# A retention-plus-GELU-MLP kernel with a build-time planner: smaller attention lead in blocks 0 and 1, a finer cut of the first product, transposes queued in the planner, a new load order

## The chip, the cores and the metric

One NeuronCore of one Trainium2 chip runs the whole program. The metric is the device time of one execution in microseconds (us). Three executions of the kernel before gave a median of 310.16 us (307.47 to 310.43). The profile is of one further execution, which took 309.51 us; its span, from the first to the last profiled instruction, is 307.7 us, so about 1.8 us lie around the span.

## The reference

The inputs are `q`, `k`, `v` of 8 batches x 8 heads x 576 positions x 64, and two weight matrices. First a retention: causal attention without softmax, each score multiplied by a decay that falls with distance. Then an MLP with exact GELU on the 4608 x 512 result.

```
scores = (q @ k^T) / 8
ret    = scores * where(i >= j, gamma[h] ** (i - j), 0)        # gamma[h] = 1 - 2 ** (-5 - h)
x      = (ret @ v), heads side by side: 4608 tokens x 512
h      = x @ w_in                                               # 512 x 2048
out    = (0.5 * h * (1 + erf(h / sqrt(2)))) @ w_out             # 2048 x 512, float32
```

## The kernel before

**Work.** The 4608 tokens are cut into 36 units of 128 tokens (all 8 heads together) and into 9 blocks of 4 units (512 tokens). Block t of the MLP needs the attention results of units 4t to 4t+3. Units 0 to 3 are the first chunks of four sequences; after that, units come in groups of two (the same chunk of two sequences), and each pair of sequences ends with a unit of two half chunks. Unit 10 is such a tail; units 11 and 12 are chunk 1 of the second pair of sequences.

**One unit.** `load` (L213, L217) brings q, k and v from HBM as bf16 by DMAs issued from GpSimd (POOL). q and k are transposed: for units 0 to 7 by TensorE (`turn`, L292, copied out of PSUM by VectorE or ScalarE), for later units by a DMA transpose issued on SyncE (`turn_dma`, L301). `scores` (L314) multiplies them, `masked` (L329, VectorE) applies the causal mask into `ret`. `scaled_v` (L339, VectorE) makes `vh`, v times a decay. `inner` (L351) multiplies `ret` with `vh` into a PSUM bank `o`. `state` (L369) sums k times `vh` over a chunk, and `cross` (L403) adds what earlier chunks contribute. `evacuate` (L423, VectorE) writes the unit's part of `xT`. Unit 2 and 3's tiles are kept aside, so VectorE scales v in the order 0, 1, 4 to 10, 2, 3, 11, 12 and so on.

**The MLP of a block.** `mlp1` (L442) is 64 matmuls of 512 columns (or 128 of 256 in blocks 0 and 1) from `xT` and `w_in`; ScalarE applies GELU into `g` (L448). `mlp2` (L481) is 64 matmuls of 512 columns from `g` and `w_out`, and the result goes out by SyncE's store (L489).

**What sets the order.** Nothing waits on a scheduler on the chip. A planner in Python writes every engine's instructions in a fixed order while the program is built. It keeps a clock per engine (`T`), a due time for each load (`land`), computed in `sw_dma` as one serial stream in which at most eight loads are outstanding, and one for each transposed unit (`s["T", j]`). At each step of its main loop it first calls `fire`, which issues loads (in the order of the list `ORDER`, then `reload`, three loads per unit), puts a `scaled_v` on VectorE as soon as the planner's clock has passed the due time of that v (and six more units than have been finished are not exceeded), and issues DMA transposes as soon as k is due. Then it takes the first attention step that is due, or else the next piece of MLP. If nothing is due before 16 us, it fills the gap with matmuls on zeros (`warm`, L565, and six at the start, L572).

On the chip each engine runs its list in order and waits on semaphores where data are late; the due times are then without effect, but the order that they gave remains. POOL's list holds the loads, SyncE's list the transposes and the stores, VectorE's list masks, `vh` and the evacuations together.

**The lead.** A new group's `scores` may be placed in the second product of a block only before two of the four pieces of each token tile, and only if the number of scored units stays within `4 * t + AHEAD`:

```
elif head is None or head[1] == 0 or head[0] == "2" and 4 <= head[3] <= 8 and head[1] < N_BLK - 1:
    if len(back) == nA - nB and (head is None or nA + len(g) <= 4 * head[1] + AHEAD):
```

With `AHEAD = 11` block 1 may score up to unit 14. The planner's window on MLP work is four runs while block 0 or 1 is at the head; a run is the list of pieces of one column range or of one group of token tiles.

## Time and profile before

| what | value |
|---|---|
| median of 3 executions | 310.16 us (307.47 to 310.43) |
| profiled execution | 309.51 us, span 307.7 us |
| TensorE matmul (PE) | busy 296.8 us, 96% of the span |
| VectorE (DVE) | busy 97.1 us, 32% |
| ScalarE (ACT) | busy 136.0 us, 44% |
| GpSimd (POOL) | busy 114.0 us, 37% |
| granted TensorE clock | 1.00 throughout |
| DMA | 35.76 MB moved, 28 transposes, mean 116 GB/s |
| first useful `mlp1` matmul | at 15.69 us |
| first `mlp1` matmul of block 2 | at 90.52 us |

How to read it: times in the views count from the start of the span. A view by time gives start, duration, engine, line, operation and tile, the number of instructions merged, and in square brackets how long the engine had been idle before and what released it. A busy share near 100% says that an engine has work, not that the work is wanted: the zero matmuls of the first 16 us count as busy. The chain of work that ended last is followed back from the end, from each instruction to what released it; a piece of it named DMA is a wait for a transfer. Idle time of an engine off this chain costs nothing.

### The profile page before, as it was taken

The page shows a single profiled execution, that of the slowest core. Times are in us where ns is not written, and L with a number is a line of the kernel's source. Part 1 is how long each engine was busy: PE and PEld are TensorE (multiplying, and loading weights), DVE is VectorE, ACT ScalarE, POOL GpSimd, SP SyncE. Part 2 cuts the span into 40 slices and gives each one's busy share as a digit, 9 for nine tenths or more (in the row PEclk, how much of TensorE's full clock was granted, in tenths as well). Part 3 has the DMA queues.
Part 4 walks back from the last instruction along what each step waited for, and adds up shares of the span by engine and source line. Part 5 has one row for each costly group of instructions (what it writes and reads, how often), then busy time and mean ns, then how long its engine had stood idle before and what let it go on. Part 6 is the DMA issues. An engine that isn't in the chain of part 4 may idle for free.

```text
span 307.7 us, 5630 instructions
## 1 busy us (share of the span) xinstructions
PE 296.8 (96%) x2354; PEld 158.9 (52%) x2354; DVE 97.1 (32%) x185; ACT 136.0 (44%) x237; POOL 114.0 (37%) x143
## 2 busy tenths in 40 slices
PE   7999999989959999999999999999999999999996
PEld 2488575855424554445445554454446444544445
DVE  6851446334543181018001851073006300400000
ACT  5286154633316622653266226631663166216611
POOL 8987899942348474105311863100000000000000
PEclk9999999999999999999999999999999999999999
DMA  9999999999999999965990999923000110010022
GB/s 142 162 191 183 177 181 214 169 151 136 169 191 186 138 156 174 194 56 86 150 159 2 167 166 174 148 69 104 34 0 36 51 54 0 36 68 34 2 60 76
DMA packets 154042, 35.76 MB, mean 116 GB/s; under 512 B 143009, under 2 KB 149537, under 8 KB 154017
## 3 DMA queue, kind: packets, MB, share of 16 engines
q0 software_dynamic: 116832, 18.10, 83.3%
q1 hardware_dynamic: 36144, 17.05, 28.8%
q8 instruction: 18, 0.29, 0.4%
q10 hardware_dynamic: 1040, 0.26, 0.4%
q14 instruction: 8, 0.06, 0.1%
HBM read 36.70 MB, written 9.44 MB: 150 GB/s over the span
## 4 chain that ended last, share of the span: by engine, by line
PE 70%; DMA 17%; POOL 10%; issue 2%; DVE 0%; ACT 0%; POOLq 0%; DVEq 0%
PE hT L442 31%; PE oT L481 30%; DMA v_ld<-in_v_dram 6%; DMA qk_ld<-in_q_dram 4%; POOL qk_ld L217 4%; DMA w_in<-in_moe_w_in_dram 3%; DMA w_out<-in_moe_w_out_dram 3%; POOL v_ld L217 3%; PE o_ps L351 2%; PE sc L314 2%; DMA qk_ld<-in_k_dram 2%; PE o_ps L403 2%; POOL w_in L191 1%; PE oT L468 1%; POOL dqT L199 1%
## 5 line engine op out<-in xcount | busy, mean ns | idle before, releaser
L442 PE MATMUL hT<-xT,w_in 128*128 128x512 bf16 (+1 forms) x704 | 127.3, 340 | 3.4 <-DVE xT L423 3.2
L481 PE MATMUL oT<-w_out,g 128*128 128x512 bf16 x560 | 126.5, 379 | 0.0
L448 ACT ACTIVATE g<-hT 128x512 bf16<-128x512 f32 x144 | 85.6, 597 | 42.3 <-PE hT L442 42.2
L442 PEld LDWEIGHTS <-w_in 128*128 128x128 bf16 x704 | 68.6, 98 | 60.4 <-issue 3.5
L481 PEld LDWEIGHTS <-g 128*128 128x128 bf16 x560 | 53.5, 98 | 60.4
L329 DVE TENSOR_TENSOR ret<-sc,msk 128x512 bf16<-128x512 f32 x56 | 35.7, 683 | 99.8 <-PE sc L314 99.8
L486 ACT COPY o_sb<-oT 128x512 f32<-128x512 f32 x35 | 20.4, 586 | 89.6 <-PE oT L481 73.0
L217 POOL DMA_DIRECT2D qk_ld<-in_q_dram x31 | 27.8, 898 | 47.0 <-PE u_ps L369 31.5
L217 POOL DMA_DIRECT2D v_ld<-in_v_dram x32 | 28.9, 906 | 8.0 <-DMA qk_ld<-in_q_dram 5.6
L282 ACT CAST u_sb<-u_ps 64x512 bf16<-64x512 f32 x31 | 18.0, 580 | 25.6 <-PE u_ps L369 24.4
L217 POOL DMA_DIRECT2D qk_ld<-in_k_dram x31 | 27.9, 900 | 3.7 <-DMA v_ld<-in_v_dram 2.9
L339 DVE TENSOR_TENSOR vh<-v_ld,dv 128x512 bf16<-128x512 bf16 x36 | 23.4, 682 | 12.4 <-DMA v_ld<-in_v_dram 12.4
L329 DVE TENSOR_TENSOR ret<-sc,near 128x512 bf16<-128x512 f32 x16 | 10.2, 682 | 35.9 <-PE sc L314 35.9
L423 DVE TENSOR_TENSOR xT<-o_ps,dqT 128x512 bf16<-128x512 f32 x28 | 18.1, 682 | 5.7 <-PE o_ps L403 5.7
L314 PE MATMUL sc<-qkT 64*128 64x128 bf16 x288 | 12.8, 223 | 2.4 <-DMA qkT<-qk_ld 2.4
L314 PEld LDWEIGHTS <-qkT 64*128 64x128 bf16 x288 | 8.3, 96 | 6.1 <-DMA qkT<-qk_ld 2.9
L351 PEld LDWEIGHTS <-vh 128*64 128x64 bf16 x224 | 6.7, 109 | 6.8 <-issue 5.9
L280 DVE COPY qkT<-qk_ps 128x512 bf16<-128x512 bf16 x13 | 5.3, 421 | 13.0 <-PE qk_ps L292 12.9
L351 PE MATMUL o_ps<-ret,vh 128*64 128x128 bf16 x224 | 9.3, 222 | 0.0
L403 PE MATMUL o_ps<-qkT,u_sb 128*128 128x128 bf16 (+1 forms) x128 | 9.1, 214 | 0.0
L213 POOL DMA_DIRECT2D v_ld<-in_v_dram x8 | 5.4, 680 | 9.4 <-DMA v_ld<-in_v_dram 3.9
L213 POOL DMA_DIRECT2D qk_ld<-in_q_dram x8 | 5.6, 706 | 4.7 <-DMA v_ld<-in_v_dram 2.2
(51 smaller groups left out, 94.1 us busy)
## 6 DMA issues: line engine op xcount, KB each, us to landing
out_dram<-o_sb SPq DMA_DIRECT2D x31, 256.0 KB, 4.6
v_ld<-in_v_dram POOLq DMA_DIRECT2D x32, 128.0 KB, 8.4
qk_ld<-in_q_dram POOLq DMA_DIRECT2D x31, 128.0 KB, 8.3
qk_ld<-in_k_dram POOLq DMA_DIRECT2D x31, 128.0 KB, 8.1
w_in<-in_moe_w_in_dram POOLq DMA_DIRECT2D x8, 256.0 KB, 7.0
w_out<-in_moe_w_out_dram POOLq DMA_DIRECT2D x8, 256.0 KB, 8.3
out_dram<-o_sb SPq DMA_DIRECT2D x9, 128.0 KB, 3.5
qk_ld<-in_k_dram POOLq DMA_DIRECT2D x8, 64.0 KB, 12.1
```

The source lines that it names most:

```text
L217: nc.gpsimd.dma_start(dst, src[2 * bp + j, :, ci * C:ci * C + C, :].rearrange("h s d -> s h d"))
L282: nc.scalar.copy(dst, src)
L314: nc.tensor.matmul(got[e][1][:, hp, :], lhsT=qkT[sl, 1, hp, :], rhs=qkT[sl, 0, hp, :], start=True, stop=True)
L329: nc.vector.tensor_tensor(r, t, by, op=ALU.mult)
L339: nc.vector.tensor_tensor(vh, loaded[i][1], dv[:, :, ci:ci + 1].to_broadcast([128, H, D]), op=ALU.mult)
L351: nc.tensor.matmul(o[64 * e:64 * e + 64, hp, :], lhsT=vals[:, 2 * hp + e, :], rhs=s["ret"][e][:, hp, :], start=(hp == 0), stop=(ci == 0 an ...
L403: nc.tensor.matmul(o[:, hp, cols], lhsT=u[:, jj, hp, :], rhs=s["qkT"][:, 0, hp, cols], start=False, stop=(hp == HP - 1), skip_group_check= ...
L423: nc.vector.tensor_tensor(dst, o, by, op=ALU.mult)
L442: nc.tensor.matmul(hT[:, m, :], lhsT=w[:, cc, o:o + 128], rhs=xT[:, cc, t * TOK + lo:t * TOK + hi], start=(cc == 0), stop=(cc == N_DM - 1))
L448: nc.scalar.activation(g_tiles[t, m0 // 2][:, m0 % 2:m0 % 2 + n, lo:hi], hT, AF.Gelu)
L481: nc.tensor.matmul(oT, lhsT=g_tiles[t, m // 2][:, m % 2, cols], rhs=w_out_sb[m // 2][:, m % 2, :], start=(m == 0), stop=(m == N_DF - 1))
L486: nc.scalar.copy(o_sb, oT)
```

## The change

Six edits, all in the planner; no instruction's operands change except the widths of the first product.

- `AHEAD` goes from 11 to 9, and 2 is added back for blocks above 1: block 0 may score 9 units and block 1 13; later blocks keep their limit.
- Block 0's first product is cut into 256, 128 and 128 columns instead of 256 and 256, so there are three runs of it in the window.
- The planner's DMA transposes are a serial queue: each takes 3.1 us after the one before and lands 3.4 us later. Before, each landed 8 us after its own issue. A transpose now delays the planner's loads by 1.6 us; before, it was 1.8 us or more.
- The planner's latency of a load goes from 4.95 to 5.2 us, and its TensorE costs are doubled up to 7.5 us (`HOT`), in place of a dearer transpose up to 9 us.
- Eight zero matmuls at the start instead of six, and a new rule for the number of those that fill gaps before 16 us.
- A new load order. k and q of unit 1 change places, v of unit 1 comes before the first weights and the constants, v of units 0 and 2 before q and k of unit 3; k and q of unit 8 come much earlier.

```diff
@@ -69,7 +69,8 @@
     N_LD = 9
     N_QKT = 8
     N_VH = 6
-    AHEAD = 11
+    AHEAD = 9
+    HOT = 7.5
 
     const = ctx.enter_context(tc.tile_pool(name="const", bufs=1))
     ld_pool = ctx.enter_context(tc.tile_pool(name="ld", bufs=N_LD))
@@ -160,6 +161,7 @@
 
 
     sw = [0.0]
+    turned = [0.0]
     flying = []
     dq_done = {1}
     land = {}
@@ -171,7 +173,7 @@
             T["pool"] = max(T["pool"], flying[-8])
         at = T["pool"]
         T["pool"] += issue
-        sw[0] = max(sw[0] + move, at + 4.95 + move - 0.9)
+        sw[0] = max(sw[0] + move, at + 5.2 + move - 0.9)
         flying.append(sw[0])
         return sw[0]
 
@@ -220,8 +222,8 @@
     tiles_of(0)
     land["q", 0], land["k", 0] = 4.5, 4.6
     cast_due = {("q", 0): (loaded[0][0][:, 0], first["q32"]), ("k", 0): (loaded[0][0][:, 1], first["k32"])}
-    ORDER = ("q1 k1 wi0 io v1 q2 k2 q3 k3 v0 v3 wi1 v2 wi2 k4 wi3 wi4 wi5 wi6 q4 v4 wo0 k5 wi7 q5 wo1 wo2 wo3 v5 k6 q6 "
-             "wo4 q7 v8 k7 dq2 wo5 wo6 q8 wo7 v7 dq3 dq4 v6 q9 k10 k9 v9 k8 q10 v10").split()
+    ORDER = ("k1 q1 v1 wi0 io k2 q2 v0 wi1 v2 k3 q3 wi2 wi3 v3 wi4 wi5 wi6 k4 q5 k5 q4 wo0 wo1 wi7 v4 v5 wo2 k6 q6 "
+             "wo3 dq2 k7 q7 wo4 k8 q8 wo5 wo6 dq3 v6 v7 wo7 v8 q9 k9 v9 dq4 q10 k10 v10").split()
 
     def next_order():
         item = ORDER.pop(0)
@@ -267,7 +269,7 @@
         if mode[0] != to:
             T["pe"] += 0.11
             mode[0] = to
-        T["pe"] += dur
+        T["pe"] += dur * (2.0 if T["pe"] < HOT else 1.0)
         return T["pe"] + DRAIN
 
 
@@ -290,7 +292,7 @@
         b, t = bank([128, HP, 128], BF16, "qk_ps")
         for hp in range(HP):
             nc.tensor.transpose(t[:, hp, :], qk[:, jj, 2 * hp:2 * hp + 2, :], ident1)
-        done = pe(0.3 if T["pe"] < 9 else 0.225)
+        done = pe(0.225)
         done = either(0.42, done, s["qkT"][:, jj], t)
         release(b, done + 0.05)
         s["T", jj] = done + SEM
@@ -300,9 +302,10 @@
         s["qkT"] = tr_pool.tile([128, 2, HP, 128], BF16, tag="qkT", name="qkT")
         nc.sync.dma_start(s["qkT"].rearrange("p j hp s -> p (j hp) s"),
                           loaded[i][0].rearrange("p j h d -> p (j h d)"), transpose=True)
-        at = on("sp", 1.3, land["k", i])
-        sw[0] = max(sw[0] + 1.8, at)
-        s["T", 0] = s["T", 1] = at + 8.0
+        at = on("sp", 1.3, max(land["q", i], land["k", i]))
+        turned[0] = max(turned[0], at) + 3.1
+        sw[0] += 1.6
+        s["T", 0] = s["T", 1] = turned[0] + 3.4
 
     def scores(i):
         s = st[i]
@@ -494,8 +497,9 @@
     runs = []
     for t in range(N_BLK):
         if t < 2:
-            for lo in (0, 256):
-                runs.append([("1", t, m, 2, lo, lo + 256) for m in range(0, N_DF, 2)])
+            cuts = (0, 256, 384, 512) if t == 0 else (0, 256, 512)
+            for lo, hi in zip(cuts, cuts[1:]):
+                runs.append([("1", t, m, 2, lo, hi) for m in range(0, N_DF, 2)])
         else:
             runs.append([("1", t, m, 1, 0, TOK) for m in range(N_DF)])
         order = range(4) if t < N_BLK - 1 else (3, 0, 1, 2)
@@ -567,7 +571,7 @@
         release(b, T["pe"])
 
     T["pe"] = 1.3
-    for _ in range(6):
+    for _ in range(8):
         b, t = bank([128, 512], FP32, "warm")
         nc.tensor.matmul(t, lhsT=zeros[:, :128], rhs=zeros, start=True, stop=True)
         release(b, 0.0)
@@ -613,7 +617,7 @@
                 if early or stuck:
                     cand(max(ready, free_time(2)) if ok else 1e9, "A", g, [])
                 elif head is None or head[1] == 0 or head[0] == "2" and 4 <= head[3] <= 8 and head[1] < N_BLK - 1:
-                    if len(back) == nA - nB and (head is None or nA + len(g) <= 4 * head[1] + AHEAD):
+                    if len(back) == nA - nB and (head is None or nA + len(g) <= 4 * head[1] + AHEAD + 2 * (head[1] > 1)):
                         cand(max(ready, free_time(min(n, 8 - len(held))) - 0.3), "A", g, back)
         if nT < N_PE_TR and nT <= nA + 3:
             key = ("qk"[half], nT)
@@ -670,8 +674,8 @@
         if not waits:
             break
         gap = min(waits) - now
-        if now < 16 and gap > 0.35:
-            warm(max(1, int(gap / 0.2158 * (0.5 if now < 9 else 0.8))))
+        if now < 16 and gap > 0.2:
+            warm(max(1, round(gap / (0.43 if now < HOT else 0.23))))
         T["pe"] = max(T["pe"], min(waits))
     assert nX == N_U and not any(runs), (nA, nB, nX, nT, nV, [len(r) for r in runs])
 
```

## The prediction

> **What bounds the kernel now.** I read the busy time by stage first, then the matmul engine's list by time, then the chain of waits. The stages:

> ```profile
> 0.00:15.70 15.70, 13.26 (x99) 5.51 (x100) 11.63 (x43) 6.30 (x16) 14.59 (x23) 1.00 1.72 153
> 15.70:65.50 49.80, 49.63 (x501) 37.02 (x500) 20.29 (x37) 27.54 (x48) 41.52 (x51) 1.00 1.87 183
> 65.50:90.50 25.00, 19.44 (x229) 10.38 (x229) 11.86 (x20) 5.82 (x10) 9.54 (x13) 1.00 1.72 162
> 90.50:305.00 214.50, 214.45 (x1528) 105.95 (x1527) 53.29 (x87) 96.11 (x163) 48.32 (x58) 1.00 0.86 94
> ```

> (Columns: stretch, length, busy time of PE, weight load, DVE, ACT, POOL, then clock, DMA share, GB/s.) From 15.7 to 65.5 and from 90.5 to the end PE has no hole. So the change can win or lose in two places alone: before 15.7, where much of PE's busy time is zero matmuls, and from 65.5 to 90.5, where 5.56 us are idle. It can also make a new hole. The idle time of the third stage, in PE's list:

> ```profile
> 65.53 0.40 PE L314 MATMUL sc<-qkT 64*128 64x128 bf16 x8
> 67.22 0.40 PE L314 MATMUL sc<-qkT 64*128 64x128 bf16 x8 [1.29 <-DMA qkT<-qk_ld]
> ...
> 77.50 0.40 PE L314 MATMUL sc<-qkT 64*128 64x128 bf16 x8 [0.25 <-DMA qkT<-qk_ld]
> ...
> 85.07 0.40 PE L314 MATMUL sc<-qkT 64*128 64x128 bf16 x8 [0.81 <-DMA qkT<-qk_ld]
> 85.40 1.90 PE L481 MATMUL oT<-w_out,g 128*128 128x512 bf16 x8
> 90.52 1.67 PE L442 MATMUL hT<-xT,w_in 128*128 128x512 bf16 x7 [3.22 <-DVE xT L423]
> ```

> Three scores come before their transposes have landed (1.29 + 0.25 + 0.81 = 2.35 us), then block 2 waits 3.22 us for an evacuation. That wait is not the evacuation's own. DVE's list, and the chain of waits:

> ```profile
> 80.29 1.28 DVE L339 TENSOR_TENSOR vh<-v_ld,dv 128x512 bf16<-128x512 bf16 x2
> 89.18 0.69 DVE L339 TENSOR_TENSOR vh<-v_ld,dv 128x512 bf16<-128x512 bf16 x1 [7.61 <-DMA v_ld<-in_v_dram]
> 89.78 1.28 DVE L423 TENSOR_TENSOR xT<-o_ps,dqT 128x512 bf16<-128x512 f32 x2
> ```

> ```profile
> 57.94 13.60 DMA qk_ld<-in_q_dram
> ...
> 72.07 17.08 DMA v_ld<-in_v_dram
> 89.15 0.02 issue
> 89.18 0.04 DVE vh L339
> ...
> 89.78 0.69 DVE xT L423
> 90.48 0.04 issue
> 90.52 13.97 PE hT L442 x64
> ```

> Counting in the order of `scaled_v`, the `vh` at 89.18 is that of unit 16, which block 2 does not need. It stands ahead of the evacuations of units 11 and 12 in DVE's list, and its v landed at 89.15. Block 2 (units 8 to 11) is pegged to the v of unit 16. **This place decides the forecast**: whatever PE gains before it is lost there unless that `vh` moves behind the evacuation of unit 11.

> **The change, part by part.**

> Start. Before the first transpose PE now has 8 zero matmuls and, by the new rule, about 3 more. (The constants move behind v of unit 1, one POOL issue of 0.9 us, so the cast of q on DVE slips from 4.90 to about 5.8.) At the 0.64 us of the row at 1.86 and 2.50, and 0.58 for the last ones, eleven end near 8.0, against 5.57 for the first transpose before: about 2.4 us later. Against it, v of unit 0, whose landing at 14.30 released the first `inner` (14.35), moves up four issues of 0.87 to 0.90 and lands near 12.4. From `inner` to the first product were 15.69 - 14.35 = 1.34 us. With scores, masks (0.685 each) and fillers after the late transposes, `inner` comes near 13.8 and the product near 15.1, 0.6 us earlier. But the weights now land later beside the loads of units 2 and 3 (second near 13.5, third 17.1, fourth 18.4, fifth 20.5, by the 1.3 us spacing of weights and 0.9 of loads in the trace), v of unit 3 near 19.2, and I find PE fully fed only from about 20. Counted by useful work done by then (transposes, scores and 24 or 26 equivalents of 256 columns), the start gains 0.2 us. Bounds: a loss of 2.6 (a planned batch of eight fillers at 0.54 instead of 0.22 each, if the clock is still low at 10 us) and a gain of 1.9 (all that v of unit 0 moves up). I take 0.2, as the fillers after 9.9 ran 0.28 apart.

> [...] Here weight loads of fillers still started 0.64 us apart at 3.78 and 4.42 although PE had worked since 1.20, and the first 0.28 apart came at 9.92. [...]

> Cut of 256, 128, 128. Half of block 0's 13.98 us becomes 128 matmuls of 128 columns. The last tile's L468 shows 32 such in about 1.80 us, 0.0563 each: 7.21 against 6.99, so +0.22 us, spent in the full stage 15.7 to 65.5. GELU pieces go from 16 x 0.597 to 8 x 0.597 + 16 at 0.37 (the copy of 256 columns took 0.37): 10.7 us in some 14, so ACT stays ahead. Sum with the start: nothing.

> Lead. Unit 13 and 14's scores (the pair at 83.86 and 85.07) leave block 1: 0.55 us of PE (16 matmuls of scores, the chain's row for a pair) moves behind the start of block 2's product. If block 2 stays pegged this is +0.55; if not, 0. Their wait of 0.81 goes with them: two blocks later the transposes (landed by 88) are there. The other two waits, 1.54, go if transposes come sooner: k of unit 8 was the last of its group (landed 51.61) and opened the queue at 54.54; it now lands near 41, so its transpose leaves about 12 us earlier, and those of units 9 to 12 start one place of 3.1 to 3.3 us sooner. SyncE's list then has a transpose ahead of the first stores, which cannot hurt at 42 since the first store went at 47.91. Bounds of this part: 0.8 to 2.35 us gained, and I take 1.9.

> The peg. `ORDER` holds the same items up to unit 10 and `reload` goes on as before, so the stream up to v of unit 16 holds the same bytes, in a DMA share that stays above 1.7. Its landing can move only by what shares the engines. From 62.63 to 89.15 landed 12 loads, 8 transposes and 3 stores; at 0.87 a load, 10.4 us; the other 16.1 us fit 1.6 per transpose and 1.1 per store. With PE some 2 us earlier, half a store more falls before it: +0.5 (bounds -1.6, one transpose less, to +3.8, one transpose and two stores more).

> Whether the `vh` still stands in front is settled in the planner's dates, which I added up by hand. They give an order, no time on the chip. Before: v of unit 16 was due at 79.58 (70.58 of loads and five transposes of 1.8), and `inner` and `state` of units 11 and 12 ended at 80.14, so it went in just ahead of `evacuate`. Now the loads sum to 70.83 and a transpose adds 1.6. With five transposes ahead of it the due time is 78.83 and `vh` stays in front; with six it is 80.43, after 80.14, and slips behind the evacuation of unit 11. Five or six hangs on whether the planner's clock takes a step between 55.53 and 56.03, when the transpose of unit 10 is due but v of unit 13 not yet called: 0.5 of a step of 0.87, so 57 to 43 for six, before what I cannot add up exactly (PE's planned clock to about 0.4).

> **The cases.** All from the profiled execution's 309.51.

> A, still pegged (0.47): 309.51 + 0.55 + 0.5 = **310.6**. Start and transpose gains only lengthen the wait at block 2, to about 6 us. Own range 308.5 to 312.

> B, `vh` behind both evacuations (0.25): 309.51 - 3.22 - 1.9 = **304.4**. For it: nothing in DVE's list needs to pass v of unit 16 until block 2's second product, 14 us later.

> B', `vh` between the evacuations of 11 and 12 (0.13): block 2 starts, but unit 12's PSUM bank stays taken until about 90.6, and of eight banks in turn it is wanted after about five pieces of 0.86: 310.6 - 4.3 = **306.3**.

> C, slower (0.15): still pegged, and the v of unit 16 lands later because stores of block 1 and a transpose, released earlier, take the engines first. Place: the wait at the start of block 2; price +3.8 - 0.5 over A: **313.9**. It decides once one more transpose and one more store than I allow land before that v. Against it: SyncE's ninth transpose waited for the k of unit 16 (86.77), which stands just before that v. [...]

> A slow start alone (up to 2.6) hides in the wait of A; with B it would give 307.

> That the planner's order hardly changes in effect is case A itself.

> **How the numbers follow.** A is the likeliest single case; near-equal chance stands against it, so the range runs from B to the foot of C: 303.9 to 312.9. It leaves out most of C and a B with all 2.35 and a faster start. The three executions stand at 307.47 to 310.43 with a median of 310.16, 0.65 above the profiled one, so A is no change from the median. About 1% is what a measurement of this kernel can tell. Faster by over 1% (under 307.1): B, B' = 0.38. Within: A = 0.47. Slower (over 313.3): C = 0.15.

> **What would show it.** In the profile after: A shows the product of block 2 at 90 to 92 with an idle time of 5 to 6 us before it, released by DVE's L423, and a `vh` just ahead that waited for a v landing at 88 to 91. B shows that product near 84 to 85, without a wait. Waits of scores for transposes between 65 and 85: gone or under 0.5. First product near 15, PE full from about 20. Scores of units 13 and 14 in block 2. The forecast is wrong if a late landing stops DVE ahead of masks instead of evacuations, or if a hole opens between 15.7 and 65.5, where I see none: there the planner's due times match the landings within 0.7 us (45.98 for 45.25 on the last weights).

## The result and the profile after

The changed kernel takes 312.09 us (median of 18 executions, 310.82 to 313.58), the kernel before 310.0 us (307.2 to 312.38) beside it: a ratio of 1.0086 with a 95% interval of 1.0058 to 1.0114. It is slower by a little under 1%. The ratios, here and below, leave out executions over 1.5% above the fastest of the same kernel, so they are not the quotients of the medians (1.0067 here). The profiled execution took 310.82 us with a span of 309.0 us, against 309.51 and 307.7 before; it is the shortest of the 18.

First the stages of the changed kernel, cut as in the prediction (length, busy time of PE, weight load, DVE, ACT, POOL, then clock, DMA share, GB/s):

```profile
15.70:65.50 49.80, 49.80 (x574) 38.04 (x572) 22.28 (x39) 26.56 (x53) 38.88 (x48) 1.00 1.85 184
65.50:90.50 25.00, 20.58 (x219) 10.69 (x218) 12.43 (x20) 6.11 (x12) 13.20 (x17) 0.93 1.85 168
90.50:306.00 215.50, 215.50 (x1539) 106.04 (x1538) 52.92 (x86) 95.95 (x163) 47.22 (x57) 0.99 0.85 92
```

PE still has no hole before 65.5 and none after 90.5. But two clock entries, in the column before the DMA share, are no longer 1.00. The matmul engine's list by time:

```profile
65.77 0.62 PE L317 MATMUL sc<-qkT 64*128 64x128 bf16 x16
...
81.25 2.75 PE L484 MATMUL oT<-w_out,g 128*128 128x512 bf16 x12
88.43 16.58 PE L445 MATMUL hT<-xT,w_in 128*128 128x512 bf16 x64 [4.42 <-DVE xT L426]
104.85 1.03 PE L484 MATMUL oT<-w_out,g 128*128 128x512 bf16 x4
```

The scores of units 8 and 9 now run as 16 matmuls in one piece, and no score waits for a transpose: the 2.35 us are gone. PE comes to block 2 at 84.0 and then stands for 4.42 us. VectorE's list says why:

```profile
87.08 0.69 DVE L342 TENSOR_TENSOR vh<-v_ld,dv 128x512 bf16<-128x512 bf16 x1 [5.67 <-DMA v_ld<-in_v_dram]
87.69 1.28 DVE L426 TENSOR_TENSOR xT<-o_ps,dqT 128x512 bf16<-128x512 f32 x2
```

It is the same place: `vh` of unit 16 stands ahead of the evacuations of units 11 and 12 and waits for its v, which landed at 87.06. After that the same 64 matmuls take 16.58 us that took 13.97 before. Here are the clock windows around that start, first of the changed kernel, then, on a grid of the same 3.41 us counted from the clock's rise at 10.53, of the kernel before. (Ahead of its rise at 10.53 the kernel before has zero matmuls starting 0.43 us apart, at 9.92 and 10.35, and behind it 0.22 us apart, at 10.88 and 11.10; in the changed kernel they are 0.43 us apart at 6.72 and 0.22 at 9.44, with the rise at 8.41. In both profiles the clock's changes lie whole multiples of 3.41 us apart: 23 of them from the rise at 8.41 to the fall at 86.92 in the changed kernel, 87 from 10.53 to 307.49, the very end, in the kernel before.)

```profile
83.51:86.92 3.41, 0.50 (x3) 0.10 (x2) 0.00 (x0) 0.59 (x1) 1.51 (x2) 1.00 1.89 140
86.92:93.75 6.83, 5.32 (x13) 1.87 (x13) 2.58 (x4) 1.20 (x3) 5.39 (x7) 0.50 1.63 177
93.75:97.16 3.41, 3.41 (x17) 1.55 (x16) 0.32 (x1) 2.38 (x4) 2.62 (x4) 1.00 2.10 158
```

```profile
85.62:89.03 3.41, 1.68 (x8) 0.69 (x7) 0.00 (x0) 0.59 (x1) 0.89 (x1) 1.00 1.65 198
89.03:92.45 3.42, 1.93 (x9) 0.87 (x9) 3.27 (x6) 0.60 (x2) 3.01 (x4) 1.00 2.01 176
```

In the changed kernel a stretch of 3.41 us with 0.50 us of work is followed by 6.83 us at half clock, which the product spends 5.3 us in and loses 2.6 us by. In the profile before, the wait of 3.22 us lay across two such stretches, each about half busy, and the clock stayed. The fall is no accident of one execution: the profiled executions below that have one stretch of 3.41 us at half clock show a mean clock of 0.994, and those with two, this one and that of the smaller lead alone, 0.989. A mean of 0.993 to 0.995 is read here as one stretch, of 0.988 or 0.989 as two. So read, 16 of the 18 executions of the changed kernel have two such stretches and two have one.

The kernel before is not free of it either, and its profile is not of its usual kind. Of its 49 executions beside the experiments below, 11 show a mean clock of 0.999 or 1.000 (median 308.81 us), 33 one of 0.993 to 0.995 (310.81 us) and 5 one of 0.989 (311.88 us). It usually loses one stretch, then, and the changed kernel two. Where the one lies no profile shows.

So the transposes' waits were won, and the wait of 4.42 us that they turned into was followed by half clock, by the mean clocks mostly for two stretches.

### The profile page after: what moved, and what is told of

The parts are those of the page before. It is cut to its first block, busy times and chain, and to the rows that moved or that the text cites. A ratio compares the mean times of both kernels' runs of the same rounds, so it can differ in the third digit from the quotient of the medians.

```text
span 309.0 us, 5788 instructions
## 1 busy us (share of the span) xinstructions
PE 300.1 (97%) x2427; PEld 161.1 (52%) x2427; DVE 98.1 (32%) x186; ACT 136.2 (44%) x244; POOL 113.8 (37%) x143
## 3 DMA queue, kind: packets, MB, share of 16 engines
HBM read 36.70 MB, written 9.44 MB: 149 GB/s over the span
## 4 chain that ended last, share of the span: by engine, by line
PE 93%; DMA 4%; DVE 1%; issue 1%; POOL 0%; ACT 0%; POOLq 0%
PE hT L445 41%; PE oT L484 36%; DMA v_ld<-in_v_dram 4%; PE sc L317 3%; PE o_ps L354 3%; PE o_ps L406 2%; PE warm L569 2%; PE warm L576 2%; PE u_ps L372 1%; PE oT L471 1%; PE qk_ps L294 1%; POOL qk_ld L219 0%; DVE qkT L282 0%; DVE vh L342 0%; DVE xT L426 0%
## 5 line engine op out<-in xcount | busy, mean ns | idle before, releaser
L445 PE MATMUL hT<-xT,w_in 128*128 128x512 bf16 (+2 forms) x768 | 130.7, 330 | 4.4 <-DVE xT L426 4.4
L451 ACT ACTIVATE g<-hT 128x512 bf16<-128x512 f32 (+1 forms) x152 | 86.5, 574 | 53.6 <-PE hT L445 53.2
L445 PEld LDWEIGHTS <-w_in 128*128 128x128 bf16 x768 | 70.4, 99 | 63.2 <-issue 8.2
L219 POOL DMA_DIRECT2D qk_ld<-in_q_dram x31 | 27.6, 891 | 49.6 <-PE u_ps L372 39.4
L219 POOL DMA_DIRECT2D qk_ld<-in_k_dram x31 | 28.0, 905 | 3.4 <-DMA v_ld<-in_v_dram 1.1
L284 ACT CAST u_sb<-u_ps 64x512 bf16<-64x512 f32 x29 | 16.8, 580 | 20.6 <-PE u_ps L372 19.4
L317 PE MATMUL sc<-qkT 64*128 64x128 bf16 x288 | 11.9, 218 | 0.1
L215 POOL DMA_DIRECT2D qk_ld<-in_k_dram x8 | 5.5, 694 | 8.7 <-DMA qk_ld<-in_k_dram 4.6
```

What stands on the lines that cost most here:

```text
L219: nc.gpsimd.dma_start(dst, src[2 * bp + j, :, ci * C:ci * C + C, :].rearrange("h s d -> s h d"))
L284: nc.scalar.copy(dst, src)
L317: nc.tensor.matmul(got[e][1][:, hp, :], lhsT=qkT[sl, 1, hp, :], rhs=qkT[sl, 0, hp, :], start=True, stop=True)
L445: nc.tensor.matmul(hT[:, m, :], lhsT=w[:, cc, o:o + 128], rhs=xT[:, cc, t * TOK + lo:t * TOK + hi], start=(cc == 0), stop=(cc == N_DM - 1))
L451: nc.scalar.activation(g_tiles[t, m0 // 2][:, m0 % 2:m0 % 2 + n, lo:hi], hT, AF.Gelu)
```

## Experiments

Each time is a median with executions of the kernel before beside it on the same chip (310.49 us in the first group, 310.67 in the second, 310.57 in the third). Ratios are to those; the changed kernel's own is 1.0086.

### The peg: one `vh` moved

The first kernel is the changed one with a single condition more; the second is the kernel before with the same condition.

```diff
-            if land["v", i] + 0.1 > now or i in kept and i + 4 > nB or nA < 4 and T["dve"] > now:
+            if land["v", i] + 0.1 > now or i in kept and i + 4 > nB or i == 16 and nX <= 12 or nA < 4 and T["dve"] > now:
```

> The changed kernel, with the vh of unit 16 placed behind the evacuations of units 11 and 12. Theory (peg and clock): block 2's product starts at 84 to 84.5 with no wait over 0.5 us, the granted clock stays at 1.00, so the wait of 4.4 us and the 2.6 us of slow product both go: 312.1 - 7.0 = 305.1 us, ratio to before about 0.984. Rival (the evacuations would be late anyway, through another item of VectorE's list or a transfer): the product still starts after 87 and the time stays above 310.

Measured: 304.78 us, ratio 0.9798 (0.9759 to 0.9836). VectorE's list of this kernel, and then PE's:

```profile
82.64 1.28 DVE L426 TENSOR_TENSOR xT<-o_ps,dqT 128x512 bf16<-128x512 f32 x2
89.21 0.69 DVE L342 TENSOR_TENSOR vh<-v_ld,dv 128x512 bf16<-128x512 bf16 x1 [5.28 <-DMA v_ld<-in_v_dram]
```

```profile
84.15 13.98 PE L445 MATMUL hT<-xT,w_in 128*128 128x512 bf16 x63
```

The `vh` waits as late as ever (89.21), but behind the evacuations; the product starts at 84.15 at full clock. The theory holds: this order on VectorE is the whole loss and more. All four executions show a clock of 1.00.

> The kernel before with the same single placement. Theory: its 3.2 us wait at the start of block 2 goes, 310.0 - 3.2 = 306.8 us, ratio about 0.99; against the changed kernel with the same placement it stays about 2 us slower, since its three waits of scores for transposes (2.35 us) remain. Rival (the wait is only moved into block 2's second product): no gain, 310.

Measured: 307.59 us, ratio 0.9888 (0.9846 to 0.993). As expected in size, but part of the wait has turned into another, a little later in PE's list and in VectorE's:

```profile
90.83 1.45 PE L442 MATMUL hT<-xT,w_in 128*128 128x512 bf16 x6 [1.67 <-DVE ret L329]
```

```profile
89.49 0.69 DVE L339 TENSOR_TENSOR vh<-v_ld,dv 128x512 bf16<-128x512 bf16 x1 [2.73 <-DMA v_ld<-in_v_dram]
90.09 2.48 DVE L329 TENSOR_TENSOR ret<-sc,msk 128x512 bf16<-128x512 f32 x4
```

With the old lead the scores of units 13 and 14 lie in block 1. Their four masks now stand behind the late `vh`, and block 2's product waits for one of them (1.67 us), as its PSUM bank is not free before. With the `vh` moved in both, the changed kernel is the faster by 2.8 us.

### The clock: the wait filled with zero matmuls

Both kernels are the changed one with n matmuls on zeros at the place of the wait, n = 16 and n = 24. They add no result and move nothing else in the planner.

```diff
             one = pick[1].pop(0)
+            if one[:3] == ("1", 2, 0):
+                t = ps.tile([128, 512], FP32, tag=frees(1)[0], name="keep")
+                for _ in range(n):
+                    nc.tensor.matmul(t, lhsT=zeros[:, :128], rhs=zeros, start=True, stop=True)
```

> The changed kernel with 16 zero matmuls (3.45 us) ahead of block 2's first product, inside its wait of 4.4 us. Theory (idle time over some 3 us halves the clock): the product still starts near 88.4, pegged, but the engine has idled only about 1 us, the clock stays at 1.00 and the product takes 14.0 instead of 16.6 us: 312.1 - 2.6 = 309.5 us. Rival (the half clock has another cause, such as the dense stretch before): the product stays slow and the time stays at 312 or rises.

Measured: 310.7 us, ratio 0.9993 (0.9953 to 1.0032), so about 0.9% under the changed kernel. In this profile v of unit 16 came 2 us later than in the one above, so 2.72 us of wait were left, and one stretch at half clock came still:

```profile
88.00:91.42 3.42, 0.90 (x5) 0.43 (x6) 1.89 (x3) 0.00 (x0) 1.99 (x3) 1.00 1.88 182
91.42:94.83 3.41, 3.41 (x10) 1.18 (x9) 0.69 (x1) 1.19 (x2) 3.41 (x5) 0.50 1.72 179
```

The expectation that 1 us would be left was wrong; that a wait of 2.7 us could still halve the clock was not in it. The "some 3 us" of its theory was the author's estimate, and no run shows such a limit. The ten executions fall into two halves: five with a mean clock of 0.994 or 0.995 took 311.12 to 312.46 us, five with 1.00 took 308.92 to 310.29 us. A later v lengthens the wait and the time at once, so not all of these 2 us need be the clock's; the next run separates the two.

> The changed kernel with 24 zero matmuls (5.2 us) ahead of block 2's product, which cover the whole wait; with 16 of them 2.7 us of it were left and one window of half clock came still. Theory (the clock falls after a stretch of 3.4 us in which the engine was mostly idle): no half clock at all after the start, product 14.0 us long, ratio to before about 1.000 or a little under, 2.6 us under the changed kernel. Rival (matmuls on zeros do not hold the clock, or it falls for another reason): a half clock near 87 to 95 again, ratio 1.005 or more.

Measured: 310.17 us, ratio 0.9976 (0.9952 to 1.0), 1.1% under the changed kernel. The wait left was 1.00 us:

```profile
84.59 5.34 PE L668 MATMUL keep<-zeros 128*128 128x512 bf16 x24
90.94 13.99 PE L445 MATMUL hT<-xT,w_in 128*128 128x512 bf16 x64 [1.00 <-DVE xT L426]
```

The product starts 2.5 us later than in the changed kernel's profile, and still the span is the same 309.0 us; all ten executions show a clock of 1.00. The clock, not the date of the start, makes the difference. The rivals (another cause, or zeros that do not count) fall.

### The lead

The kernel before with the smaller lead alone, and the changed kernel with the old lead.

```diff
-    AHEAD = 11
+    AHEAD = 9
-                    if len(back) == nA - nB and (head is None or nA + len(g) <= 4 * head[1] + AHEAD):
+                    if len(back) == nA - nB and (head is None or nA + len(g) <= 4 * head[1] + AHEAD + 2 * (head[1] > 1)):
```

> The kernel before with the smaller lead alone (9, and 11 above block 1). Theory: the scores of units 13 and 14 leave block 1 with their 0.81 us wait, so the engine reaches block 2 about 1.4 us earlier and waits 4.6 instead of 3.2 us for the same landing; the clock halves, block 2's product takes 2 to 2.6 us longer, and 0.55 us of scores come later: about 313, ratio 1.010. Rival (the lead costs only the moved scores, as forecast): 310.6, ratio 1.002.

Measured: 310.82 us, ratio 1.0019 (0.998 to 1.0058): the rival's figure. Yet its profile has the theory's mechanism: the wait is 4.23 us, 6.83 us of half clock follow, and the product takes 16.83 us.

```profile
88.84 16.83 PE L442 MATMUL hT<-xT,w_in 128*128 128x512 bf16 x63 [4.23 <-DVE xT L423]
```

In that execution v of unit 16 landed 1.7 us earlier than in the profile before, which pays for part of it. That the median does not rise by 2 us fits the clocks of the other executions: of the ten, five show 0.989, four 0.993 or 0.994 and one 1.00, while of the 19 of the kernel before beside them one shows 0.989, twelve 0.993 to 0.995 and six 0.999 or 1.00. That is two thirds of a stretch more per execution, about 1.1 us (an estimate, at half of 3.41 us a stretch), which the interval allows. The theory left out that the kernel before loses a stretch too.

> The changed kernel with the old lead (11) alone. Theory: the scores of units 13 and 14 return to block 1, 0.55 us of work and a wait of 0.5 to 1 us for the transpose of unit 14, so the engine idles about 3 us at the same pegged start; the half clock comes in some runs only, and 0.55 us less work stands behind: 312.1 - 0.55 - 1 to 2.6 = 309 to 310.5, ratio 0.998 to 1.002. Rival (the loss comes from the load order or the start): the time stays at 312, ratio 1.007 or more.

Measured: 309.27 us, ratio 0.9986 (0.9932 to 1.0041), as the theory has it, with a mean clock of 0.994 in six of eight executions and of 1.00 in two. PE's list and the clock stretches show another way of losing:

```profile
84.40 0.40 PE L317 MATMUL sc<-qkT 64*128 64x128 bf16 x8 [2.28 <-DMA qkT<-qk_ld]
```

```profile
81.28:84.69 3.41, 1.13 (x24) 0.79 (x23) 0.69 (x1) 1.16 (x2) 1.28 (x3) 1.00 1.57 199
84.69:88.11 3.42, 3.42 (x12) 1.19 (x9) 0.50 (x1) 0.00 (x0) 1.27 (x3) 0.50 1.83 145
```

The score of unit 14 waits 2.28 us for its transpose, the clock halves during the second product of block 1, and the evacuation is then in time for block 2, at 88.98. While the peg is there, the smaller lead therefore costs the changed kernel about 1%: it takes away work and a wait that had shortened the one at block 2. On the kernel before its cost (1.0019) is not clear of noise.

### The start

The changed kernel with the `vh` of unit 16 behind, and once with the cut of block 0 undone, once without the fillers before the first transpose.

```diff
-            cuts = (0, 256, 384, 512) if t == 0 else (0, 256, 512)
+            cuts = (0, 256, 512)
```

```diff
-        if now < 16 and gap > 0.2:
+        if 6 < now < 16 and gap > 0.2:
```

> The changed kernel with the vh of unit 16 placed behind and block 0's first product again in 256 and 256 columns. It tells what the finer cut is worth once nothing downstream swallows it. Theory: with units 2 and 3 as one piece the engine runs out of weights between 16 and 21 us; the cut is worth about 1 us net of its 0.2 us, so this run is near 305.8 (ratio 0.983). Rival (the cut only costs its 64 extra matmuls): 304.6, ratio 0.979.

Measured: 306.01 us, ratio 0.9823 (0.9796 to 0.985). By the medians the cut is worth 1.2 us, near the theory's 1; but the intervals with and without it overlap, and this profile has a wait of 1.20 us at block 3, where the `vh` of unit 22 waited for its v, so its worth is not shown. The weights do run out, as the theory said, but the wait for them is 0.31 us, at 19.50.

> The changed kernel with the vh of unit 16 placed behind and without the three fillers before the first transpose (eight zero matmuls at the start remain). Theory: the first transpose leaves at about 6.4 instead of 7.6 us, and the chain to the first product, pinned by v of unit 0 (12.6 us), gains 0.3 us at most: 304.5, ratio 0.979. Rival (the fillers buy an earlier full clock): the clock rises one window later and the start loses 1 to 1.5 us: 306, ratio 0.984.

Measured: 306.62 us, ratio 0.9848 (0.9801 to 0.9895), the rival's figure and again not its reason. The first product came at 14.85 (15.09 with the fillers) and the full clock came later: two zero matmuls at 9.18 still took 0.92 us, while with the fillers two at 9.74 took 0.60. In the profiled execution (308.51 us, the longest of the four) the loss is a second peg, one block on:

```profile
117.78 0.69 DVE L342 TENSOR_TENSOR vh<-v_ld,dv 128x512 bf16<-128x512 bf16 x1 [4.11 <-DMA v_ld<-in_v_dram]
118.39 1.28 DVE L426 TENSOR_TENSOR xT<-o_ps,dqT 128x512 bf16<-128x512 f32 x2
```

This `vh`, of unit 22, stands ahead of the evacuations of units 15 and 16; block 3 waited 3.04 us for them and then had 3.41 us of half clock. In the run with the fillers the same `vh` ran at 115.14, just in time. The other three executions took 305.31, 305.73 and 307.5 us with a clock of 1.00, and the interval overlaps that of the run with the fillers, so what the fillers are worth is not shown.

### The order on VectorE as a rule

Four kernels take the place of unit 16's condition by a rule: the changed kernel, the kernel before, the changed one with the old lead, and the kernel before with the smaller lead.

```diff
                 break
+            t = runs[0][0][1] if runs and runs[0] else 0
+            if t and i >= 4 * t + 12 and nX < max(4 * t + 8, nB):
+                break
             scaled_v(i)
```

> The changed kernel with the placement as a rule: while block t is at the head, no vh of a unit from 4t+12 on goes into VectorE's list before the units of block t+1, and all that have had their inner product, are evacuated. One profile with the single placement still had a 3.0 us wait and a half clock at block 3, behind the vh of unit 22; the rule moves that one too. Theory: no wait of PE over 0.5 us from 16 us to the end, no half clock after the start, 304 us, ratio 0.979 or a little under. Rival: the vh only come to stand ahead of masks and hold PSUM banks, 306 or more.

Measured: **304.01 us**, ratio 0.9792 (0.974 to 0.9844), 303.5 to 304.33 over four executions. PE has no hole in the third stage:

```profile
65.50:90.50 25.00, 25.00 (x245) 13.03 (x244) 12.43 (x20) 9.99 (x17) 12.20 (x16) 1.00 1.86 168
```

This beats both kernels, by some 6.5 us and 8 us. Against the single placement (304.78 us) the intervals overlap.

> The kernel before with the same rule. Theory: as with the single placement, 307.6 (ratio 0.989 to 0.990), since the masks of units 13 and 14, still scored in block 1, stand behind the vh of unit 16 and hold their PSUM banks (1.7 us of wait seen at block 2), and the scores still wait for transposes (some 1.8 us). Rival: the rule alone brings all of it, 305.

Measured: 307.24 us, ratio 0.9898 (0.9814 to 0.9981), as the theory has it: waits of 0.73, 0.46 and 0.59 us for transposes and 1.47 us for a mask are left.

> The changed kernel with the rule and the old lead of 11. Theory: scoring units 13 and 14 in block 1 costs a wait for the transpose of unit 14 (2.3 us seen in the run with the lead undone) and puts their masks behind the vh of unit 16, so block 2 meets banks that are still held: 306.5 to 308, ratio 0.987 to 0.992. Then the smaller lead is worth 2 to 3 us once the order on VectorE is mended. Rival: the lead is worth nothing, 304.

Measured: 308.46 us, ratio 0.9934 (0.9895 to 0.9973), a little worse than the theory's 0.987 to 0.992, and in its profile (310.26 us, one of the longer of 306.25 to 310.61) by its first reason alone. The score of unit 14 waits 3.52 us for its transpose, and the 12 matmuls behind it take 5.29 us, where the changed kernel's take 2.75, in an execution with a mean clock of 0.989:

```profile
85.56 0.61 PE L317 MATMUL sc<-qkT 64*128 64x128 bf16 x8 [3.52 <-DMA qkT<-qk_ld]
86.10 5.29 PE L484 MATMUL oT<-w_out,g 128*128 128x512 bf16 x12
```

Held banks do not show. With the order on VectorE mended, the smaller lead is worth about 4 us in the changed kernel, the opposite of its effect with the peg.

> The kernel before with the rule and the smaller lead, without the other parts of the change. Theory: the wait for banks goes with the lead (1.7 us) and one of the waits for transposes (0.7), which leaves one of about 0.5 to 1.1 and the old start: 305.5, ratio 0.983. What then separates it from the changed kernel with the rule (0.979) is the worth of the order, the queue of transposes and the start together. Rival: equal to it, so that these are worth nothing.

Measured: 305.61 us, ratio 0.9845 (0.9783 to 0.9906), near the theory's 305.5. One wait of 1.33 us for a transpose and one of 1.1 us for weights are left in its profile; the kernel with the whole change has neither. By medians the rest of the change is worth 1.6 us, and the smaller lead alone 1.6 us (307.24 without it), but in both cases the intervals overlap.

## Why the forecast came out as it did

Case A, "still pegged", was the likeliest and is what happened; the time, 312.09, lies inside the stated range of 303.9 to 312.9, but 0.1 us above this case's own (308.5 to 312) and 1.5 us above its 310.6. The range held it because it reached towards case C; nothing in it stood for what cost the time. The direction, which it called no change, is slower by 0.9%, within the bound of 1% that it named. That A was called likeliest is in part luck: the planner's dates, as the forecast worked them, gave 57 to 43 for the `vh` slipping behind, yet A and C together, with the `vh` in front, got 0.62, and no step leads from the one to the other.

- **The peg** held as worked out: `vh` of unit 16 in front of unit 11's evacuation, as five transposes ahead of it in the planner's dates would have it, and not six; the dates themselves no run shows. With that one `vh` moved, nothing else holds block 2 of the changed kernel (a wait of 0.2 us is left).
- **The transposes' waits**: 1.9 us forecast, 2.35 us gone. With the peg, all of it lengthened the wait at block 2, from 3.22 to 4.42 us, and not to the 6 us forecast, since v landed earlier.
- **The start**: first product forecast near 15.1, came at 14.79; PE full from about 20 forecast, but from 16 on it has no hole. Its net gain was put at 0.2 us, less 0.22 for the cut. The score of unit 8, after the same work, came at 65.53 before and at 65.77 after. In the nine profiles with the new load order it comes at 65.77 to 66.52, in four of the five with the old one at 65.31 to 65.53 and in the fifth at 67.36: nothing gained, near the sum, and mostly some tenths lost. One reading in the working was wrong: 0.28 us is the idle time before the weight load at 9.92, not the distance of two, and those matmuls still started 0.40 to 0.43 us apart; the clock rose at 10.53.
- **The landing of unit 16's v**: the term of +0.5 us cannot be judged. In the pair of profiles the landing moved from 89.15 to 87.06, by -2.1 us, 0.5 beyond the lower bound of -1.6 that the forecast gave: the transpose of unit 15 and a store landed after it now, not before. But over all profiles it lies at 87.47 to 90.46 in the five kernels with the old load order and at 87.06 to 90.41 in the nine with the new one, and the profile of the changed kernel has the earliest of all. Whether the change moves it is not shown.
- **The missing term**: the sum for A has no price for a longer wait. "Start and transpose gains only lengthen the wait at block 2" is the step that failed. A longer wait is not free: it halved the clock for 6.83 us and cost 2.6 us in the profile; filling it brought the ratio from 1.0086 to 0.9976. With -2.1 for the landing and +0.55 for the moved scores, these make the 1.3 us by which the span grew, to 0.3. The 309.51 from which the forecast started is an execution without half clock; against the usual one the price is one stretch more, 1.7 us (an estimate, half of 3.41), and with the 0.55 that comes to some 2.3 us, beside the 2.1 us between the medians.
- **Case C** named the right side with the wrong mechanism: the loss is not a later landing.

The forecast reckoned with the clock at the start alone. The profiles show 3.41 or 6.83 us at half clock in later stages, and up to 1.13 us of work in a stretch did not hold the full clock there. The low clock that the trace of the kernel before shows at the start, with zero matmuls 0.43 us apart where later ones are 0.22 apart, should have been held against every wait that the change could lengthen.

## What to carry to other kernels

A late operand blocked all that stood behind it in VectorE's list: one `vh` waited 5.67 us for its v, and block 2's product 4.42 us for the evacuations behind it. So put work that no one needs yet behind what the next stage waits for, rather than trust the date at which its data should be there. Work and waits taken out ahead of that pegged start only lengthened the wait, from 3.22 to 4.42 us in the profiles, and the longer wait was followed by 6.83 us at half clock: price the waits that remain as well as those that go. Try a change such as the smaller lead again once the wait behind it is mended; in the changed kernel it cost 1% with the peg and gained over 1% without.

## What the runs showed of the hardware that was not expected

A wait of 2.28 us was followed by half clock, and one of 3.22 us, in the profile before, was not. What went with the clock in these runs is how much work fell into one stretch of 3.41 us, on a grid that took no notice of where a wait began: in the changed kernel the stretch that decided started at 83.51, 22 such lengths after the clock's rise at 8.41, and the wait at 84.00.

| kernel | longest wait | work in the stretch that decided | clock after it |
|---|---|---|---|
| before, as profiled | 3.22 us, across two stretches | 1.68 and 1.93 of 3.41 us | 1.00 |
| changed, lead undone | 2.28 us | 1.13 us | half for 3.41 us |
| changed, 16 zero matmuls in the wait | 2.72 us | 0.90 us | half for 3.41 us |
| changed | 4.42 us | 0.50 us | half for 6.83 us |
| changed, 24 zero matmuls in the wait | 1.00 us | not under 2.4 us | 1.00 |
